# First batch of a fused attention and feed-forward kernel: four neighbouring tokens per partition, loads by pairs of heads, turned head by head with products

## Chip, cores, metric

One core of one Trainium2 chip. The metric is the time of the whole program on the device in microseconds (us), taken outside the profiler. A profile's span is about 1.8 us shorter than that time. The engines are called PE (matrix products; PEld is its weight load), ACT (scalar engine), DVE (vector engine) and POOL. Every comparison below is between runs of the fast state, with one exception that is named (a single run, e6).

## The reference, cut to what matters

```python
# x: (8, 8, 512, 64) batch, head, token, depth;  state: (8, 8, 32, 64);  all float32
scores  = x @ state.T / 8        ; a  = softmax(scores)  ; xread = a  @ state
scores2 = state @ x.T / 8        ; a2 = softmax(scores2) ; sread = a2 @ x
attn = concatenate([xread, sread], axis=tokens)          # 512 + 32 rows per batch
h = attn.reshape(4352, 512) @ w_in                       # w_in 512 x 2048, given as float64
out = (h * erf(softplus(h))) @ w_out                     # w_out 2048 x 512, float64
```

The weights come as float64 and are turned into float32 on the chip by ACT and DVE, step by step, while batch 0 is already in work. The order of tokens within a batch is free as long as the stores put the rows back.

## The kernel before, the parts that matter

Names: `st` is the state, `xT` is x turned so that a pair of heads (2 x 64) lies on the 128 partitions, `warm(n)` issues n products of the identity with itself, which keep PE busy. A plain product is two passes in the trace, a transpose one.

```python
x_t[0] = xin.tile([P, NC, H, D], F32, name="x")            # token 128*c + p on partition p
for c in range(NC):                                        # four quarters of the tokens
    (nc.scalar, nc.sync)[c % 2].dma_start(
        out=x_t[0][:, c], in_=x[0, :, P * c:P * c + P].rearrange("h p d -> p h d"))
for e in range(2):
    nc.sync.dma_start(out=st[:, 0, D * e:D * e + D], in_=...)
# ... then three weight loads of 1 MB on the sync queue, then warm(8)

def scored(b, xT):                                         # 8 products of 64*32 tiles, 512 columns
    s2 = [ps_at.tile([P, S], F32, name="at") for _ in range(2)]
    for i in reversed(range(NI)):
        for e in range(2):
            r, q = slice(D * e, D * e + D), slice(Ns * i, Ns * i + Ns)
            nc.tensor.matmul(out=s2[e][q, :], lhsT=st[r, b, q], rhs=xT[r, i, :], ...)
    return s2

def attention0(between):
    ...
    for c in 1, 0, 2, 3:
        if c == 2:
            warm(3)
        for i in range(NI):
            nc.tensor.transpose(out=xp[i][:, P * c:P * c + P],
                                in_=xt[:, c, 2 * i:2 * i + 2, :], identity=ident)
    for i in range(NI):
        (nc.scalar.copy, nc.vector.tensor_copy)[i % 2](xT[:, i, :], xp[i])
    states(range(1), ps_h, "h")                            # turn the state, copy by ACT
    s2 = scored(0, xT)
    between[0]()                                           # warm(32), first weight steps on ACT
    ...
    a = states_weights(0, s2, both)                        # DVE: transposes, maxima, ...
```

## Time and profile before

| | before |
|---|---|
| time, 4 runs | 732.15 us median (732.14 to 732.36) |
| span of the profiled run | 730.7 us |
| PE busy | 721.6 us (99%) |
| DVE busy from 11.5 to 31 us | 19.07 of 19.5 us |
| DVE's first transpose of scores starts | 11.57 us |
| first long group of PE products starts | 31.01 us |

### The profile page before, as it was taken

What the parts mean: (1) busy time and instruction counts of PE and PEld (TensorE: products, weight loads), DVE (VectorE), ACT (ScalarE), POOL (GpSimd) and SP (SyncE); (2) the same over time, 40 slices, a digit from 0 to 9 for tenths busy, and PEclk for the clock granted to TensorE, in tenths of its full rate; (3) what the DMA queues carried; (4) which work ended last, traced back from release to release, by engine and by line L of the source; (5) the groups of instructions that cost most, each with busy time, mean ns of one, the idle gap of its engine ahead of it and who ended that gap; (6) DMA issues with size and microseconds to landing.
All of it is one profiled execution on the core that took longest, in us unless ns stands there. A gap on an engine that the chain in (4) does not pass through costs nothing.

```text
span 730.7 us, 12128 instructions
## 1 busy us (share of the span) xinstructions
PE 721.6 (99%) x5016; PEld 588.0 (80%) x5016; DVE 524.0 (72%) x766; ACT 395.6 (54%) x498; POOL 0.7 (0%) x6
## 2 busy tenths in 40 slices
PE   8899999999999999999999999999999999999998
PEld 7434435889889888988989888988898899999996
DVE  4988887997798677867587669866686756674423
ACT  4898894665556444754455445544575434443340
POOL 0000000000000000000000000000000000000000
PEclk9999999999999999999999999999999999999999
DMA  7577842330153203310061104220111000000001
GB/s 234 174 216 241 224 94 58 87 59 30 19 99 67 50 1 66 80 30 30 1 144 27 33 1 94 60 44 9 38 50 30 30 1 30 1 30 1 30 1 29
DMA packets 139166, 46.40 MB, mean 64 GB/s; under 512 B 126696, under 2 KB 130536, under 8 KB 139112
## 3 DMA queue, kind: packets, MB, share of 16 engines
q1 hardware_dynamic: 136840, 44.92, 24.6%
q10 hardware_dynamic: 2272, 0.72, 0.5%
q8 instruction: 39, 0.64, 0.4%
q14 instruction: 15, 0.12, 0.1%
HBM read 33.03 MB, written 8.91 MB: 57 GB/s over the span
## 4 chain that ended last, share of the span: by engine, by line
PE 92%; DVE 2%; ACT 1%; issue 0%; ACTq 0%
PE o L600 50%; PE h L493 27%; PE o L550 7%; PE at L407 2%; PE h L407 1%; PE h L714 1%; PE at L197 1%; PE at L421 1%; PE h L277 1%; DVE s L727 0%; PE at L277 0%; DVE hs L721 0%; ACT L724 0%; DVE w_out L148 0%; ACT s L724 0%
## 5 line engine op out<-in xcount | busy, mean ns | idle before, releaser
L600 PE MATMUL o<-w_out,s 128*128 128x256 f32 x480 | 118.0, 380 | 0.0
L600 PE MATMUL o<-raw,hs 128*128 128x256 f32 x480 | 117.3, 382 | 0.0
L500 ACT ACTIVATE s<-hs 128x512 f32<-128x512 f32 x120 | 75.4, 630 | 74.3 <-DVE hs L501 74.0
L600 PE MATMUL o<-w_out,hs 128*128 128x256 f32 x480 | 114.1, 380 | 0.0
L600 PEld LDWEIGHTS o<-raw,hs 128*128 128x128 f32 x480 | 89.9, 190 | 22.6 <-issue 10.9
L501 DVE TENSOR_TENSOR hs<-hs,h 128x512 f32<-128x512 f32 x90 | 61.8, 687 | 62.6 <-PE h L493 62.4
L600 PEld LDWEIGHTS o<-w_out,hs 128*128 128x128 f32 x480 | 90.8, 190 | 16.3 <-issue 4.2
L600 PEld LDWEIGHTS o<-w_out,s 128*128 128x128 f32 x480 | 84.6, 191 | 7.9
L501 DVE TENSOR_TENSOR hs<-s,h 128x512 f32<-128x512 f32 x60 | 41.1, 685 | 67.6 <-PE h L493 67.1
L493 PEld LDWEIGHTS h<-aT,m 128*128 128x128 f32 x672 | 83.8, 192 | 4.3 <-issue 1.4
L493 PE MATMUL h<-aT,m 128*128 128x128 f32 x672 | 84.4, 275 | 0.0
L545 DVE TENSOR_TENSOR s<-s,hs 128x2048 f32<-128x2048 f32 (+1 forms) x31 | 68.8, 2218 | 20.4 <-ACT s L543 20.4
L504 ACT COPY s<-h 128x512 f32<-128x512 f32 x29 | 17.0, 585 | 107.7 <-PE h L493 107.7
L550 PE MATMUL o<-w_out,s 128*128 128x512 f32 x128 | 59.1, 600 | 0.6 <-DVE s L727 0.5
L493 PE MATMUL h<-sy,sx 128*128 128x128 f32 x448 | 59.4, 275 | 0.0
L493 PEld LDWEIGHTS h<-sy,sx 128*128 128x128 f32 x448 | 56.7, 192 | 2.1 <-issue 0.5
L543 ACT ACTIVATE s<-s 128x2048 f32<-128x2048 f32 x30 | 57.4, 1912 | 0.3
L509 ACT COPY hs<-h 128x512 f32<-128x512 f32 x29 | 17.0, 585 | 74.8 <-PE h L493 74.8
L600 PE MATMUL o<-raw,s 128*128 128x256 f32 x240 | 56.8, 379 | 0.0
L550 PEld LDWEIGHTS o<-w_out,s 128*128 128x128 f32 x128 | 23.1, 190 | 31.1 <-issue 25.8
L600 PEld LDWEIGHTS o<-raw,s 128*128 128x128 f32 x240 | 43.5, 190 | 4.7
L500 ACT ACT_TABLE_LOAD x31 | 39.8, 1283 | 0.5
(133 smaller groups left out, 915.4 us busy)
## 6 DMA issues: line engine op xcount, KB each, us to landing
raw<-in_moe_w_in_dram SPq DMA_DIRECT2D x8, 1024.0 KB, 5.7
raw<-in_moe_w_out_dram SPq DMA_DIRECT2D x8, 1024.0 KB, 4.8
xq<-in_x_dram SPq DMA_DIRECT2D x112, 64.0 KB, 2.2
x<-in_x_dram SPq DMA_DIRECT2D x56, 128.0 KB, 2.8
out_dram<-ot SPq DMA_DIRECT2D x18, 256.0 KB, 2.2
sc<-xT SPq DMA_DIRECT2D x112, 32.0 KB, 1.9
out_dram<-ot SPq DMA_DIRECT2D x28, 128.0 KB, 1.9
x<-in_x_dram ACTq DMA_DIRECT2D x2, 256.0 KB, 5.7
```

The lines of the kernel that those rows point to most:

```text
L197: on_pe = nc.tensor.matmul(out=s2[e][q, :], lhsT=st[r, b, q], rhs=xT[r, i, :], start=True, stop=True)
L277: nc.tensor.matmul(out=sr[q, e, :], lhsT=a2T[:, e, c, q], rhs=xt[:, c, 2 * i + e, :], start=(c == 0), stop=(c == NC - 1))
L407: nc.tensor.matmul(out=ps[k][e][q, :], lhsT=st[r, b, q], rhs=w_in[r, 2 * g:2 * g + 2, i, :], start=True, stop=True)
L493: last = nc.tensor.matmul(out=bank[:, q], lhsT=lhsT, rhs=rhs, start=(first and i == 0 and k == 0), stop=(i == GF - 1 and k == len(ops) - 1 ...
L500: nc.scalar.activation(out=s[:, k], in_=hs[:, k], func=ACTF.Softplus)
L501: add = lambda o, x, y: nc.vector.tensor_tensor(o, x, y, op=ALU.add)
L504: copy(m1, p)
L509: copy(c11, p)
L543: nc.scalar.activation(out=s, in_=s, func=ACTF.Erf)
L545: nc.vector.tensor_tensor(s[:, k], s[:, k], hs[:, k], op=ALU.mult)
L550: nc.tensor.matmul(out=acc[r], lhsT=gT[:, i, P * r:P * r + P], rhs=w_out[:, GF * g + i, :], start=(g == 0 and i == 0), stop=(g == NG - 1 a ...
L600: nc.tensor.matmul(out=acc[bank][:, E2 * c:E2 * c + E2], lhsT=lhs[:, i, :], rhs=rhs[:, g, i, :], start=(first and i == 0 and c == 0), stop ...
```

## The change

Its intent: each token's 64 numbers are 256 B, so the old load moved x in 4096 pieces of 256 B. With tokens 4p to 4p+3 on partition p, a head gives 1 KB per partition in one piece. Loading by pairs of heads also lets the first pair be turned, copied and scored while later pairs arrive. In the new layout the two heads of a token no longer lie side by side, so a transpose of 128 columns can't take them together, and each head is turned by a product with the identity.

```diff
-    x_t[0] = xin.tile([P, NC, H, D], F32, name="x")
-    for c in range(NC):
-        (nc.scalar, nc.sync)[c % 2].dma_start(
-            out=x_t[0][:, c], in_=x[0, :, P * c:P * c + P].rearrange("h p d -> p h d"))
-    for e in range(2):
-        nc.sync.dma_start(out=st[:, 0, D * e:D * e + D], in_=...)
+    x_t[0] = xin.tile([P, H, NC, D], F32, name="x").rearrange("p h c d -> p c h d")
+    def load_x0(queue, h, n):
+        queue.dma_start(out=x_t[0][:, :, h:h + n, :].rearrange("p c h d -> p h c d"),
+                        in_=x[0, h:h + n].rearrange("h (p c) d -> p h c d", c=NC))
+    for k in range(2):
+        for j, queue in enumerate((nc.scalar, nc.sync)):
+            load_x0(queue, 4 * k + 2 * j, 2)
+            if k == 0:
+                load_st0(queue, j)
 ...
-    def scored(b, xT):
+    def scored(b, xT, s2=None, pairs=tuple(reversed(range(NI)))):
 ...
-        (the loop over c with its 16 transposes, the four copies, states, scored(0, xT))
+        def turn(i):
+            for c in range(NC):
+                for e in range(2):
+                    nc.tensor.matmul(out=xp[i][D * e:D * e + D, P * c:P * c + P],
+                                     lhsT=xt[:, c, 2 * i + e, :], rhs=ident, start=True,
+                                     stop=True)
+            (nc.scalar.copy, nc.vector.tensor_copy)[i % 2](xT[:, i, :], xp[i])
+        turn(0)
+        turn(1)
+        states(range(1), ps_h, "h")
+        warm(2)
+        turn(2)
+        scored(0, xT, s2, (0, 1))
+        turn(3)
+        warm(2)
+        scored(0, xT, s2, (2, 3))
 ...
-        rows = out[TB * b:TB * b + S].rearrange("(c p) e -> c p e", p=P)
+        rows = out[TB * b:TB * b + S].rearrange("(p c) e -> c p e" if b == 0 else
+                                                "(c p) e -> c p e", p=P)
```

More of the change, by code (lines that the diff above doesn't have):

```diff
@@ L106, with load_st0 @@
     st = const.tile([P, B, P], F32, name="st")
-    x_t[0] = xin.tile([P, NC, H, D], F32, name="x")
-    for c in range(NC):
-        (nc.scalar, nc.sync)[c % 2].dma_start(
-            out=x_t[0][:, c], in_=x[0, :, P * c:P * c + P].rearrange("h p d -> p h d"))
-    for e in range(2):
-        nc.sync.dma_start(out=st[:, 0, D * e:D * e + D],
-                          in_=state[0].rearrange("(i e) n d -> e i n d", e=2)[e])
+    x_t[0] = xin.tile([P, H, NC, D], F32, name="x").rearrange("p h c d -> p c h d")
+    def load_x0(queue, h, n):
+        queue.dma_start(out=x_t[0][:, :, h:h + n, :].rearrange("p c h d -> p h c d"),
+                        in_=x[0, h:h + n].rearrange("h (p c) d -> p h c d", c=NC))
+    def load_st0(queue, e):
+        queue.dma_start(out=st[:, 0, D * e:D * e + D],
+                        in_=state[0].rearrange("(i e) n d -> e i n d", e=2)[e])
+    for k in range(2):
[3 more added lines that the diff above has]
+                load_st0(queue, j)
     def load_st():
@@ L188 @@
     marks = []
-    def scored(b, xT):
-        s2 = [ps_at.tile([P, S], F32, name="at") for _ in range(2)]
-        for i in reversed(range(NI)):
+    def scored(b, xT, s2=None, pairs=tuple(reversed(range(NI)))):
+        s2 = s2 or [ps_at.tile([P, S], F32, name="at") for _ in range(2)]
+        for i in pairs:
             for e in range(2):
@@ L299, in attention0 @@
         xp.append(ps_h.tile([P, S], F32, name="h"))
-        for c in 1, 0, 2, 3:
-            if c == 2:
-                warm(3)
-            for i in range(NI):
-                nc.tensor.transpose(out=xp[i][:, P * c:P * c + P],
-                                    in_=xt[:, c, 2 * i:2 * i + 2, :], identity=ident)
-        for i in range(NI):
+        s2 = [ps_at.tile([P, S], F32, name="at") for _ in range(2)]
+        def turn(i):
[4 more added lines that the diff above has]
+                                     stop=True)
             (nc.scalar.copy, nc.vector.tensor_copy)[i % 2](xT[:, i, :], xp[i])
+        turn(0)
+        turn(1)
         states(range(1), ps_h, "h")
-        s2 = scored(0, xT)
+        warm(2)
[4 more added lines that the diff above has]
+        scored(0, xT, s2, (2, 3))
         between[0]()
```

## The prediction

> **What bounds the kernel now.** I read the page first, then the stretches by engine, then the order of time of the first 32 us, then the waits, because the change touches only the load, the turn and the scores of batch 0, and the stores' row order. The page's head says what those can be worth at all:
>
> ```profile
> span 730.7 us, 12128 instructions
> PE 721.6 (99%) x5016; PEld 588.0 (80%) x5016; DVE 524.0 (72%) x766; ACT 395.6 (54%) x498; POOL 0.7 (0%) x6
> ```
>
> PE is busy for all but 9 us. A change before the first full stretch of PE work can only move that stretch earlier or later as a whole. The stretches (start and end; length; busy us of PE, PE weight load, DVE, ACT, POOL; clock; DMA share; GB/s) show where slack is:
>
> ```profile
> 11.50:31.00 19.50, 17.34 (x122) 11.61 (x122) 19.07 (x27) 15.97 (x21) 0.00 (x0) 1.00 0.52 184
> 31.00:52.00 21.00, 20.80 (x76) 8.57 (x77) 18.25 (x20) 19.17 (x23) 0.00 (x0) 1.00 0.73 220
> 52.00:130.00 78.00, 77.52 (x423) 35.71 (x422) 63.96 (x91) 60.33 (x87) 0.00 (x0) 1.00 0.57 149
> ```
>
> From 11.5 to 31 us DVE is the bound: 19.07 of 19.5 us, and the waits of DVE in that window hold nothing but the wait that starts it. PE is not the bound there: 64 of its 122 passes are fillers on the identity that keep its clock up. From 31 us PE is the bound. So the end is set by when DVE begins its first transpose of scores, at 11.57 us. What leads there, in order of time (start, length, engine, line, operation, count, idle before):
>
> ```profile
> 1.35 3.78 PE L169 MATMUL o<-ident 128*128 128x128 f32 x16 [1.35 <-POOL ident masks.py:199]
> 4.92 0.86 PE L304 MATMUL o<-ident,x 128*128 128x128 f32 x3
> 6.64 0.98 PE L169 MATMUL o<-ident 128*128 128x128 f32 x6
> 7.95 0.33 PE L304 MATMUL o<-ident,x 128*128 128x128 f32 x1 [0.32 <-DMA x<-in_x_dram]
> 9.47 0.68 DVE L307 COPY xT<-h 128x512 f32<-128x512 f32 x1
> 10.30 1.09 PE L197 MATMUL at<-xT,st 64*32 64x512 f32 x16 [0.78 <-DVE xT L307]
> 11.57 1.31 DVE L217 STREAM_TRANSPOSE xT<-at 128x512 f32<-128x512 f32 x2 [1.42 <-PE at L197]
> ```
>
> The reader should see three things. The last token quarter of x lands at 7.94 us and PE has waited for it (0.32 us, after a filler of 1 us): the start is DMA-bound at that point. From there to 11.57 it is a serial chain: 8 transposes, copies, scores. And a plain product counts two passes in the trace (warm(8) is x16), a transpose only one.
>
> **What the Trainium skill says.** (1) "TensorE: Matmul & The Clock Gate", section "Part 1: The HAM clock gate", gives half clock until about 3.4 us of sustained work. The trace agrees in kind: the fillers and the first transposes run at about 0.21 us per 128-column pass, later ones at 0.107 to 0.12, and the filler count per 0.2 us goes from 2 to 4 at about 7.0 us, although the granted clock reads 1.00 throughout. (2) "TensorEngine Tiling (Array Packing)", section "Feature Incompatibilities": column tiling excludes transpose mode for fp32, which is why turning heads one at a time must be done with products; its "Key Properties" say that changing the tiling mode drains the array. The trace shows such a cost: the weight combination between two 128*128 groups has 2 x 0.213 = 0.43 us of streaming per tile but takes 0.59, so about 0.08 us a switch. (3) "DMA: Bandwidth & Descriptors", section "Why small descriptors are slow (HBM only)": a 256 B descriptor pays 27% overhead. In the trace, x in 256 B pieces moves at 217 to 290 GB/s between 3 and 7 us, and the weights in 2 KB pieces at 400 to 430 between 9 and 14 us.
>
> **The change part by part.**
>
> Load. Four tokens per partition make each head's piece 1 KB instead of 256 B: 1024 pieces instead of 4096, for the same 1 MB and four transfers. Before, the transfers land at 4.83 us (issue 0.73 plus the shortest 4.1 to landing) to 7.94 us. Interpolating the time of a packet between 256 B and 2 KB at the two rates above, 1 KB pieces give some 370 to 390 GB/s (estimate). With first bytes at about 2.2 us as before, the first two pairs land about 4.4 to 4.8 us and the last two about 5.7 to 6.2. The data come about 2 us earlier, the first weight transfer too, since less is ahead of it. That takes the 7.94 wait away.
>
> Turn. 16 transposes (16 passes of 128 columns, over all 128 array columns) become 32 products (64 passes of 128 columns, each on half the columns). Two halves run side by side if the array treats them as it does the narrower products: in the read of tokens, 64 passes of 64 columns on 128*32 tiles take
>
> ```profile
> 87.48 1.03 PE at L277 x64
> ```
>
> where 64 x 0.053 = 3.4 us would be serial and a quarter is 0.85; so tiles do run together, plus some 0.18. For one turn of a pair: 16 passes / 2 x 0.107 = 0.86 us warm, 1.7 us cold. Four turns are 3.4 us warm against 16 x 0.122 = 1.95 us for the transposes: **PE's own work in the opening rises by 1.5 us**, more where it is cold. Copies are the same four, three of them now hidden.
>
> Scores. They split into two halves of 8 passes. Before, all eight tiles of 64*32 run together: 2 x 0.43 plus fill is 1.09. Each half still has two passes per tile of 0.43, so each half costs 0.86 plus fill: **one score time becomes two**, the first ahead of the last turn on PE.
>
> PE is in order, so I add its queue from the end of the unchanged fillers at 5.13 us:
> - turn 0, cold: 8 x 0.213 = 1.7, ends 6.85
> - turn 1, nearly all warm: 0.95, ends 7.8
> - switch, states' transpose and warm(2) (4 passes): 0.65, ends 8.45
> - turn 2 with a switch: 1.0, ends 9.45 (its data landed at about 6, no wait)
> - scores of pairs 0 and 1 with a switch: 0.95, ends 10.4
> - turn 3 with a switch: 1.0, ends 11.4
> - copy of the last pair on DVE: 0.1 to start plus 0.69, ends 12.2 (warm(2) lies beside it)
> - scores of pairs 2 and 3: 0.1 plus 1.05, ends 13.3; DVE begins at about 13.4
>
> Against 11.57 that is **+1.8 us**. The path no longer runs over DMA but over PE.
>
> Does the shift reach the end? DVE has no idle from 11.57 to 31 us, so it moves as a block; its weight steps wait for ACT's conversions, which come earlier with the data and not later. After 31 us PE idles 0.2 us in 21 and 0.5 us in 78, too little to absorb 1.8. The 64 filler passes move along (13.3 to 20.7) and end before the product at 19.64 + 1.8 that follows them. The stores of batch 0 go to rows four apart, but each row is still a 2 KB piece. The later read of x in its new layout still takes 64 contiguous numbers. So the sum: 732.15 + 1.8 = **733.95**, which I call 733.9.
>
> **The rivals.**
>
> (A) The gain is kept: the author's idea is that turns, copies and scores of early pairs hide under the loads, and that only one turn, one copy and half the scores follow the last landing. That tail is 1.0 + 0.8 + 1.15 + 0.15 = 3.1 us against 11.57 - 7.94 = 3.6 now. If PE were free at the last landing (6 us) DVE would begin about 9.1 and the time be 729.7; if PE is partly in the way, 731. Against it: PE's queue above contains nothing that waits for data after 5.1, and its tile-bound minimum without switches, 1.7 + 3 x 0.86 + 0.86 + 0.5 + 0.8 + 1.05, already puts DVE past 12.6.
>
> (B) The two halves of the array don't overlap in these products, for instance because the two passes of one product have to go in order: turns then cost 3.4 cold and 1.86 warm. The queue becomes 5.1, 8.3, 10.2, 10.8, 12.8, 13.7, 15.6, and DVE begins at about 17.5 (part of turn 0 warm saves 0.5): +5.5, 737.6. Against it stands the read of tokens, whose passes come in the same order and do overlap. For it: I have no row of a 128*64 tile.
>
> (C) The clock comes up one window later or earlier than 7.0 us. Before, PE waited for data at that time and was insensitive. Now turn 1 (and 2) would run cold: +0.9 to +1.7, so about 735.2; if earlier, -0.8, so 733.1.
>
> (D) The first pair lands later than 5.1 us, say 5.8, because the state pieces and two queues mix: all of PE's queue moves by 0.7, 734.6.
>
> **Range and chances.** I give the main sum, with (C) and (D) as its spread, some 75%, A 15%, B 10%. The 8-in-10 range is 732.0 to 735.8: below it lies most of A, above it B and the worst of C. A 2% verdict needs 14.6 us, the whole of the opening up to the scores and more; so within 2% is all but sure: faster 0.005, same 0.985, slower 0.01.
>
> **What would show each step.** In the profile after: x landing by about 6.2 us, with 350 GB/s or more in 3 to 5 us (load); no PE wait for x after the first turn; the turn's 16 passes taking 0.9 to 1.0 us warm and about 1.8 cold (overlap; 1.9 and 3.4 would be B); the last score half beginning near 12.3 with the last copy as its releaser; DVE's first transpose near 13.4, and the first long PE group of 24 passes, now at 31.01, near 32.8. The prediction is wrong in its sum if DVE's first transpose comes before 11.6, in its mechanism if PE waits there for x, and in its passing-on if DVE's start and that PE group move by different amounts or if the span moves by less than they do.

## The result and the profile after

| | before | after |
|---|---|---|
| time, 4 runs | 732.15 us (732.14 to 732.36) | 734.86 us (733.97 to 735.66) |
| span of the profiled run | 730.7 | 733.0 |
| DVE's first transpose of scores starts | 11.57 | 13.96 |
| first long group of PE products starts | 31.01 | 33.37 |

Ratio 1.0036, 95% interval 1.0019 to 1.0053. (A ratio is the mean time of one kernel's fast runs over the mean of the other's of the same rounds, so not quite the ratio of the medians.) The changed kernel is slower by 2.7 us, and its runs spread over 1.7 us, where those of the kernel before spread over 0.2.

The changed kernel in order of time (start, length, engine, line, operation, count, idle before). These lines answer to those of before in the prediction:

```profile
5.07 3.16 PE L314 MATMUL o<-ident,x 128*64 128x128 f32 x32
8.16 0.33 PE L191 MATMUL h<-ident,st 128*128 128x128 f32 x1
8.86 1.09 PE L314 MATMUL o<-ident,x 128*64 128x128 f32 x16
9.89 1.06 PE L206 MATMUL at<-xT,st 64*32 64x512 f32 x8
10.88 1.09 PE L314 MATMUL h<-ident,x 128*64 128x128 f32 x16
12.02 0.69 DVE L317 COPY xT<-h 128x512 f32<-128x512 f32 x1 [3.05 <-PE h L314]
12.54 0.36 PEld L206 LDWEIGHTS at<-xT,st 64*32 64x32 f32 x8
12.55 1.27 PE L206 MATMUL at<-xT,st 64*32 64x512 f32 x8
13.96 1.31 DVE L226 STREAM_TRANSPOSE xT<-at 128x512 f32<-128x512 f32 x2 [1.24 <-PE at L206]
...
33.37 1.12 PE L568 MATMUL o<-w_out,s 128*128 128x512 f32 x2 [0.24 <-DVE s L746]
```

Before, PE waited for the last quarter of x until 7.94 us. In this trace no PE line carries a wait for x: PE goes from turn to scores to turn without a gap. The one late wait of the opening is DVE's 3.05 us for the last turn. The copy of that turn ends at 12.71, 2.56 us after the last copy of before (9.47 + 0.68 = 10.15).

The stretch that follows, from each kernel's start of the DVE block, is nearly a copy of that of before. DVE is busy 18.69 of 19.5 us (about 0.46 us of this stretch lies ahead of the block's start), and it waits for nothing between 13.96 and the first long PE group:

```profile
13.50:33.00 19.50, 17.63 (x126) 11.80 (x122) 18.69 (x26) 13.42 (x19) 0.00 (x0) 1.00 0.34 114
```

So in this trace the loss is made entirely in the first 14 us: 13.96 - 11.57 = 2.39 us there, 33.37 - 31.01 = 2.36 at the first long PE group, 733.0 - 730.7 = 2.3 at the end.

### The profile page after: what moved, and what is told of

It reads as the page before. It is cut to its first block, busy times and chain, and to the rows that moved or that the text cites. A ratio compares the mean times of both kernels' runs of the same rounds, so it can differ in the third digit from the quotient of the medians.

```text
span 733.0 us, 12227 instructions
## 1 busy us (share of the span) xinstructions
PE 725.1 (99%) x5066; PEld 590.2 (81%) x5066; DVE 524.1 (71%) x766; ACT 395.6 (54%) x498; POOL 0.7 (0%) x6
## 4 chain that ended last, share of the span: by engine, by line
PE 90%; DVE 3%; ACT 2%; issue 1%; DVEq 0%; ACTq 0%
PE o L618 49%; PE h L511 27%; PE o L568 7%; PE at L425 2%; PE h L425 1%; PE h L733 1%; PE at L206 1%; PE at L439 1%; PE h L286 1%; DVE s L746 0%; PE at L286 0%; DVE hs L740 0%; ACT L743 0%; DVE w_out L157 0%; DVE xT L357 0%
```

## The experiments

Twelve kernels ran on the chip, and all gave the reference's result. "DVE start" is the start of DVE's first transpose of scores in that run's trace. Times are medians with the lowest and highest in brackets; "before" is that of the same rounds. The rounds ran on four chips (e1 to e4; e5 to e8; e9 to e11; e12); their medians of before lie between 732.33 and 732.36, so runs of different rounds are compared directly. The diffs below are shortened.

| run | what | time | before | DVE start | first long PE group | span |
|---|---|---|---|---|---|---|
| e1 | the changed kernel again | 734.73 (734.07 to 735.03) | 732.36 | 14.06 | 33.47 | 733.1 |
| e2 | new tokens, pairs kept side by side, transposes | 732.65 (732.15 to 732.82) | 732.36 | 10.94 | 30.36 | 730.4 |
| e3 | changed loads, regrouping copies, transposes | 733.69 (731.73 to 735.30) | 732.36 | 14.46 | 33.93 | 733.5 |
| e4 | changed, scores undivided | 733.58 (732.81 to 733.80) | 732.36 | 12.81 | 32.22 | 731.9 |
| e5 | changed, x on one queue | 734.11 (733.85 to 734.73) | 732.35 | 13.18 | 32.63 | 732.3 |
| e6 | changed, state loads last (one run) | 735.41 | 732.35 | 14.55 | 33.97 | 733.6 |
| e7 | e3 with x on one queue | 731.33 (730.78 to 731.41) | 732.35 | 10.51 | 29.97 | 729.6 |
| e8 | e7 with 256 B pieces | 731.97 (731.83 to 732.07) | 732.35 | 10.99 | 30.43 | 730.1 |
| e9 | e5, scores undivided | 733.43 (732.49 to 733.55) | 732.33 | 12.59 | 32.04 | 731.7 |
| e10 | e5, turns ordered by head | 735.70 (735.22 to 736.22) | 732.33 | 14.52 | 33.95 | 733.6 |
| e11 | before, x on one queue | 732.13 (732.05 to 732.51) | 732.33 | 11.19 | 30.61 | 730.2 |
| e12 | e7, states behind x | 730.65 (730.61 to 731.31) | 732.34 | 9.64 | 29.13 | 728.9 |

Read the last three columns first. In these twelve traces and the two of before and after, the long PE group starts 19.41 to 19.49 us after DVE's start. The span ends 719.0 to 719.5 us after it. Whatever an experiment does to the opening, the end moves by the amount by which DVE's start moves, within 0.13 us of before's 719.13. The exception is e2, 0.33 longer: its shift is still whole at DVE's last instruction (726.44 us against 727.09), and 0.3 us is lost after it, in the last stores. From here on, only the way to DVE's start is asked about.

The two theories at the outset: the loss is **PE's own added work** (four times the passes for the turns, each on half the array, and the scores twice), partly run at half clock; or it is **something else the change brought** (the token order, the loads, the stores).

### e1: the changed kernel again

No edit.

> The changed kernel itself, to learn its spread and where its tensor clock comes up. My theory: the first turns of the changed kernel run partly at half clock, and the moment at which the clock comes up (about 7.0 us in the profile before, about 7.5 in the profile after) differs from run to run; each us that it comes later costs half a us. So the runs spread between about 733.9 and 735.7, while the kernel before, which waits for data until 7.94 us, stays within 0.3 of 732.15. In this run's trace the start of DVE's first transpose of scores minus 11.57 equals the span minus 730.7 within 0.1 us. Rival (the spread is chance of the chip and hits both kernels, or comes after the opening): the kernel before spreads as much, or the span and DVE's start do not move together.

The spread came back (1.0 us here, against 0.4 for 11 runs of before on the same chip), and the span followed DVE's start: +2.49 and +2.4. The first two turns, the same 32 passes from the same start, took different times in different traces of this code. After, e1, e5 (which differs only in its queues):

```profile
5.07 3.16 PE L314 MATMUL o<-ident,x 128*64 128x128 f32 x32
```
```profile
5.06 2.60 PE L314 MATMUL o<-ident,x 128*64 128x128 f32 x32
```
```profile
5.06 2.23 PE L313 MATMUL o<-ident,x 128*64 128x128 f32 x32
```

The stretches of PE alone (start and end, length, busy and passes touched, clock, DMA share, GB/s) show why. In the profile after, two equal stretches of 0.4 us at 5.6 and 6.6 us hold the same few passes, and only the one at 7.6 holds more:

```profile
5.60:6.00 0.40, 0.40 (x8) 1.00 1.06 371
6.60:7.00 0.40, 0.40 (x8) 1.00 1.05 407
7.60:8.00 0.40, 0.40 (x12) 1.00 1.05 410
```

while in e5 a faster rate is there already at 6.4:

```profile
5.20:5.60 0.40, 0.40 (x6) 1.00 1.03 318
6.40:6.80 0.40, 0.40 (x14) 1.00 1.05 404
```

The rate doubled at about 7.5 us after, 6.5 in e1 and 5.8 in e5, read from where the pass count rises in stretches of 0.2 us; this document calls it the clock coming up, though the "1.00" in the clock column shows none of it. It can come earlier still: in e11 and e12 the first fillers, the same 16 passes that take 3.78 us elsewhere, were shorter, and the rate doubled at about 4.2 and 4.6 us:

```profile
1.35 3.40 PE L169 MATMUL o<-ident 128*128 128x128 f32 x16 [1.35 <-POOL ident masks.py:199]
1.35 3.58 PE L177 MATMUL o<-ident 128*128 128x128 f32 x16 [1.35 <-POOL ident masks.py:199]
```

What was not expected is a second source of spread: e1 had its first turns done 0.56 us earlier than the profile after, yet its DVE started 0.1 us later. PE waited for the third pair of x, which had not landed before 8.97 us:

```profile
8.97 1.09 PE L314 MATMUL o<-ident,x 128*64 128x128 f32 x16 [0.59 <-DMA x<-in_x_dram]
```

That load was issued on the scalar queue at 2.43 us, so it took 6.5 us. Between 7 and 8 us the sync queue (q1) moves weights with nearly all engine time, and the scalar queue (q10) still has 23 packets under way (packets, MB, share of the engines):

```profile
q1 hardware_dynamic: 167, 0.33, 93.2%
q10 hardware_dynamic: 23, 0.02, 5.2%
```

### e2: the new tokens without the products

```diff
-    x_t[0] = xin.tile([P, H, NC, D], F32, name="x").rearrange("p h c d -> p c h d")
+    x_t[0] = xin.tile([P, NC, H, D], F32, name="x")      # loads head by head
-  32 products                                            # in turn(i)
+  nc.tensor.transpose(out=xp[i][:, P*c:P*c+P], in_=xt[:, c, 2*i:2*i+2, :], identity=ident)
-  warm(2), scored (0, 1), warm(2), scored (2, 3)
+  warm(2), scored (0, 1, 2, 3) once, at the end
```

> Four tokens per partition kept, but the tile keeps the heads of a token side by side, so that pairs of heads are turned by 16 transposes as before (one pass each), scores undivided, no fillers after the first eight; loads head by head, with 256 B pieces on the chip's side. My theory (PE's own added work is what costs): the last head lands at about 7 to 8 us, DVE's first transpose of scores starts at 10.5 to 11.5, time 731.1 to 732.1, and the spread is small again. Rival (the new token order or the order of loads costs by itself, for instance through the stores to every fourth row): 734 or more although the products are gone.

DVE started at 10.94, inside the expected window, and the profiled run took 732.16. The median of 732.65 missed the expected 731.1 to 732.1: it is level with before, ratio 1.0003 (0.9991 to 1.0016). The small spread did not come either (0.67 us). The rival is out: with the new token order, the new stores and the order by pairs all kept, the 2.4 us are gone. (The expectation said no fillers after the first eight; in fact one warm(2) stayed.) The simplest version, transposes on the changed layout, does not build (it never ran): the build refuses a stationary operand with more than one free dimension, and two heads 1 KB apart have two. That, and not only the column tiling that the prediction named, is why the change needs products.

### e3: the changed loads, two heads laid side by side by copies

```diff
+  xg = act.tile([P, 4, S], F32, name="hs")
+  for i in range(NI):
+      (nc.vector.tensor_copy, nc.scalar.copy)[i % 2](
+          xg[:, i].rearrange("p (c e d) -> p c e d", c=NC, e=2), xt[:, :, 2*i:2*i+2, :])
-  32 products
+  nc.tensor.transpose(out=xp[i][:, P*c:P*c+P], in_=xg[:, i, P*c:P*c+P], identity=ident)
-  the fillers and the divided scores
+  scored(0, xT, s2, (0, 1, 2, 3)) once, at the end
```

> The changed loads exactly (1 KB pieces by pairs of heads), then DVE and ACT, idle at that time, copy each pair so that its two heads lie side by side, and 16 transposes and undivided scores follow. My theory: pairs land at 4.3 to 6 us, copies of 0.4 to 0.7 us end by about 6.7, transposes end at about 7.5, DVE's first transpose of scores starts at 9.5 to 10.3: time 730.1 to 730.9, faster than both. Rival (DMA still bounds, or what DVE starts earlier is lost again because the first weights are not converted): DVE's start may be earlier but the time is 732 or more, with a new wait on ACT or the weight transfer in the DVE block.

A miss, and the most useful one. The runs lie between 731.73 and 735.30. The trace is of the slowest, and DVE's copy of the third pair shows what it stood on:

```profile
9.69 0.43 DVE L319 COPY hs<-x 128x512 f32<-128x512 f32 x1 [4.67 <-DMA x<-in_x_dram]
```

The third pair, issued on the scalar queue at 2.72, landed at 9.69, while the fourth, on the sync queue, was there by 7.05. PE then stood idle for 2.92 us. Of the eight transposes left, four still ran at the high rate (0.66 us) and four at the low one (0.99), and the scores took 2.73 us. So the sentence in the prediction that the last two pairs land at 5.7 to 6.2 us is wrong. The profile after shows it too, in its times from issue to landing: the third pair was issued at 2.44 us and took 5.1, so it landed at about 7.5. Only, PE was not ready for that pair before 8.86 there, so that nothing waited.

### e4: the scores undivided

```diff
-        scored(0, xT, s2, (0, 1))
         turn(3)
         warm(2)
-        scored(0, xT, s2, (2, 3))
+        scored(0, xT, s2, (0, 1, 2, 3))
```

> The changed kernel with the scores in one piece after the last turn. My theory: a half of the scores costs PE as much as the whole (two passes of 0.43 us per tile), so the first half's 1.0 us leaves the queue and nothing comes in its place but the switch of mode: DVE starts 0.8 to 1.1 us earlier than in the changed kernel, time 733.8 to 734.1 at the same clock. Rival (the halves run half as long, and the first half is hidden as was meant): the time rises by 0.3 to 0.5.

1.15 us faster than e1 in the median (733.58 against 734.73), with DVE's start 1.25 us earlier. The rival is out: dividing the scores costs and hides nothing. The undivided scores take as long in the trace as one half does in the profile after:

```profile
11.40 1.27 PE L206 MATMUL at<-xT,st 64*32 64x512 f32 x16
```

### e5 and e6: which queue, and what stands last in it

e5: the four loads of x on the sync queue, in order, both state loads on the scalar queue. e6: on each queue both loads of x, then one state load.

```diff
-    for k in range(2):
-        for j, queue in enumerate((nc.scalar, nc.sync)):
-            load_x0(queue, 4 * k + 2 * j, 2)
-            if k == 0:
-                load_st0(queue, j)
+    for j in range(4):                      # e5
+        load_x0(nc.sync, 2 * j, 2)
+    for j in range(2):
+        load_st0(nc.scalar, j)
```

> The changed kernel with all four loads of x on the sync queue, in order and ahead of the first weights, and both state loads on the scalar queue. Theory W: in the changed kernel the third pair lands late (8.97 us in e1, 8.86 in e4, 9.69 in e3) because on the scalar queue it shares the engines with the first weights of the sync queue. Then here all pairs land by 5.8 us, PE never waits for x after the first turn, and DVE's start is set by PE alone: 13.4 to 14.0 depending on when the clock comes up, time 733.9 to 734.8, with a smaller spread; so it stays slower than before by 1.6 to 2.4 us, because PE's queue is the bound. Rival: the transfers are slow by themselves with this layout; the last pair then lands at 8 us or later here too.

> The changed kernel with both x loads of each queue ahead of the state load, so that the third pair is issued on the scalar queue at about 1.3 us instead of 2.4 us. Theory W (shared with the weights): its bytes are asked for before the weights, so it lands by about 6, one look 733.9 to 734.9. Rival L (a load on the scalar queue is late whatever is issued when): it lands at 7.5 us or later, as before.

e5: no wait for x any more; the longest of the four loads took 4.8 us to land instead of 6.5. The expected landing of all pairs by 5.8 us did not come: the last load, issued at about 2.3, landed at about 7.1, before PE needed it. The median fell by 0.62 us against e1 and stayed 1.76 above before. So the late third pair is worth up to 0.6 us (the runs of e1 and e5 overlap; PE's wait for it was 0.59 us in e1's trace, 0.26 in e4's and nothing in the profile after), and the rest is PE. The expected smaller spread did not come: 0.9 us against 1.0, which leaves the clock as the likely main source of the spread (argued from the turns' lengths above, not forced by an experiment).

e6: the third pair, now issued at about 1.3 us, made PE wait no more; no load of x took more than 5.0 us. The late one was now the state, last on the scalar queue:

```profile
8.76 0.33 PE L191 MATMUL h<-ident,st 128*128 128x128 f32 x1 [1.12 <-DMA st<-in_state_dram]
```

So it is not x or its layout that is slow. What stood last on the scalar queue while the sync queue had a megabyte of weights in flight landed late, and the time with it (735.41, a single run, above the expected 733.9 to 734.9). That the weights are what delays it is argued: no run takes them away.

### e7 and e8: the regrouping copies with the loads put right, and the size of the pieces

e7 is e3 with e5's queues and all four copies on DVE. e8 is e7 with "(c p)" in place of "(p c)" in the load and in the stores, so the pieces are 256 B again.

> e3 (1 KB pieces, copies that lay pairs of heads side by side, 16 transposes) with x on the sync queue ahead of the weights, and all four copies on DVE. Theory: pairs land at 3.6 to 5.7 us, copies of 0.43 us end by 6.2, PE turns from 5.1 to 7.8 or 8.7 (depending on the clock) without a gap, DVE's first transpose starts at 9.8 to 10.7: 0.9 to 1.8 us less than before of the same chip, so 730.5 to 731.4, and a spread well under that of e3 (3.6 us). Rival: DVE's start comes that early but the span follows by less, because the first weights (landing near 10 us or later) then hold up the DVE block.

> e7 with the old assignment of tokens to partitions, so that x moves in 256 B pieces again; nothing else differs. Theory (the piece size is what the four tokens per partition buy): 1 MB at 220 to 290 GB/s, so the last pair lands at 6.6 to 7.4 instead of 5.7, DVE's start is 0.7 to 1.5 us later than in e7. Rival (the load is latency and issue, not pieces): within 0.3 us of e7.

e7 beats before: 731.33 against 732.35, ratio 0.9983 (0.9970 to 0.9996), DVE's start at 10.51. The time fell by 1.02 us, as DVE's start did (1.06 against the 11.57 of before), so the rival (first weights in the way) is out. ACT did wait 0.91 us for the first weights, but DVE needs them only at 14.10.

e8 is 0.64 us slower than e7, and no run of one reaches into those of the other. DVE's start is 0.48 later: less than the expected 0.7 to 1.5, more than the rival's 0.3. So the piece size counts, for less than was thought. Between 3 and 6 us all transfers together moved 308, 264 and 360 GB/s in e7, and 267, 223 and 218 in e8. The last row of e7 holds the first weights, in 2 KB pieces; of x alone, the sync queue moved 0.54 MB in e7 and 0.44 in e8 between 3 and 5 us:

```profile
3.00:4.00 1.00, 1.00 (x6) 1.00 (x6) 0.39 (x1) 0.82 (x1) 0.00 (x0) 1.00 1.07 308
4.00:5.00 1.00, 1.00 (x7) 1.00 (x6) 0.30 (x2) 0.00 (x0) 0.00 (x0) 1.00 0.85 264
5.00:6.00 1.00, 1.00 (x7) 1.00 (x6) 0.47 (x2) 0.00 (x0) 0.00 (x0) 1.00 1.07 360
```
```profile
3.00:4.00 1.00, 1.00 (x6) 1.00 (x6) 0.00 (x0) 0.79 (x1) 0.00 (x0) 1.00 1.21 267
4.00:5.00 1.00, 1.00 (x7) 1.00 (x6) 0.43 (x1) 0.00 (x0) 0.00 (x0) 1.00 1.26 223
5.00:6.00 1.00, 0.74 (x6) 0.51 (x4) 0.43 (x1) 0.26 (x1) 0.00 (x0) 1.00 1.27 218
```

### e9 and e10: the two terms of PE's queue, with the loads out of the way

e9 is e5 with e4's edit. e10 is e5 with the loops of a turn exchanged:

```diff
-            for c in range(NC):
-                for e in range(2):
+            for e in range(2):
+                for c in range(NC):
```

> e5 (changed kernel, x on one queue) with the scores undivided, as in e4. Theory: the first half of the scores (1.0 us plus switches) leaves PE's queue and, since no wait for x takes its place, the time falls by 1.0 to 1.3 us against e5: 732.8 to 733.2. Rival (part of e4's gain of 1.15 us was the clock or the late pair): it falls by less than 0.8.

> e5 with the products of a turn ordered by half of the array (all four of one head, then all four of the other), so that neighbours on PE's queue use the same half. Theory (overlap needs neighbours on different halves; e5's turns take 8 x 0.107 us because heads alternate): a warm turn costs about 1.7 instead of 0.95 us, the two cold ones together about 5 instead of 2.2 to 3.2, so DVE starts 2.5 to 4 us later: 736.6 to 738.1. Rival (PE pairs them in whatever order within a turn): no change against e5, 734.1 within 0.5.

Against e5, e9 fell by 0.68 us only, by the medians: below the expected 1.0 to 1.3, and by that measure the rival's case. Its trace, however, had a late clock: the first two turns took 2.95 us, against 2.23 in e5's. Read from PE's queue, where the clock is up in both, the term is there in full. From the start of turn 2 to the start of turn 3 it is 2.01 us in e5 (8.09 to 10.10) and 0.93 in e9 (8.64 to 9.57), so the half scores cost 1.08 us. What is left, 1.1 us above before with neither divided scores nor a wait for x, is put down to the products.

e10 slowed by 1.59 us against e5, less than the expected 2.5 to 4 and far from the rival's nothing. A turn at the high clock, from its start to that of the scores behind it, takes 1.51 us in e10 and 1.02 in e5. The first group is of e10, the second of e5:

```profile
8.47 1.58 PE L313 MATMUL o<-ident,x 128*64 128x128 f32 x16
9.98 0.63 PE L205 MATMUL at<-xT,st 64*32 64x512 f32 x4
```
```profile
8.09 1.09 PE L313 MATMUL o<-ident,x 128*64 128x128 f32 x16
9.11 0.63 PE L205 MATMUL at<-xT,st 64*32 64x512 f32 x4
```

Sixteen passes one after the other would be 16 x 0.107 = 1.71 us and a full overlap 0.86, each plus a switch. So alternating halves overlap nearly fully, and with four neighbours on the same half some overlap remains. How PE arranges that stays open. Part of the miss is the clock, too: it came up early in that trace, at about 5.5 us, so the first two turns together took 2.77 us and not about 5.

### e11: the kernel before with only its queues changed

```diff
-        (nc.scalar, nc.sync)[c % 2].dma_start(out=x_t[0][:, c], ...)
+        nc.sync.dma_start(out=x_t[0][:, c], ...)
-        nc.sync.dma_start(out=st[:, 0, D * e:D * e + D], ...)
+        nc.scalar.dma_start(out=st[:, 0, D * e:D * e + D], ...)
```

> The kernel before with only its queues changed: all four loads of x on the sync queue, the states on the scalar queue. Theory (e7's gain comes from the earlier landing that 1 KB pieces and the queue give, at equal work of PE): the last 256 B quarter lands at about 7.2 to 7.9 us as in e8, where the last copy waited until 7.88, so the time is within 0.4 of before. Rival (the queue alone is worth e7's 1.0 us): 731.4 or less.

732.13 against 732.33, ratio 0.9999 (0.9985 to 1.0012): the queue alone is worth little, and the rival is out. The last quarter landed at 8.0 us, just outside the expected window. Of e7's 1.0 us, the queue alone gives 0.2 (e11) and the queue with the copies but 256 B pieces 0.4 (e8); the larger pieces without the queue made it slower in the median (e3, whose copies were also shared with ACT).

### e12: nothing on the second queue

```diff
-        load_st0(nc.scalar, j)
+        load_st0(nc.sync, j)                # behind the four loads of x
         turn(1)
-        states(range(1), ps_h, "h")
         turn(2)
         turn(3)
+        states(range(1), ps_h, "h")
```

> e7 with the state loads behind x on the sync queue (nothing on the scalar queue at all) and the states' transpose behind the four turns. In e7 the fourth pair landed at 7.00 us and the states at 7.37, PE waiting 0.55 us for them. Theory (two queues in flight at once delay whichever is last in its own): the fourth pair lands by 6 us, PE has no gap, and DVE starts at 9.8 to 10.3 instead of 10.51: time 730.5 to 731.1. Rival (the states' smaller pieces then land after 8 us, just before the scores): DVE's start as in e7 or later, 731.3 or more.

730.65, ratio to before 0.9979 (0.9966 to 0.9993): the fastest of all. DVE's start came at 9.64, a little before the expected window. The fourth pair was copied from 6.53 us on instead of 7.00, later than the expected 6, and PE still has gaps: 0.53 us for the third pair at 6.33 and 0.35 for the state's copy. The scores run undivided. Two queues in flight were the theory; this trace also has the earlier clock shown under e1, so how much of the 0.68 us between e7 and e12 is the queue is not shown. Its lines:

```profile
6.53 0.43 DVE L318 COPY hs<-x 128x512 f32<-128x512 f32 x1 [0.26 <-DMA x<-in_x_dram]
8.24 1.26 PE L205 MATMUL at<-xT,st 64*32 64x512 f32 x16 [0.35 <-ACT st L191]
9.64 1.31 DVE L225 STREAM_TRANSPOSE xT<-at 128x512 f32<-128x512 f32 x2 [1.24 <-PE at L205]
```

## Why the prediction held, and where it was off

The main sum was slower by 1.8 us. Measured were 2.7 us (first rounds) and 2.4 us (e1), inside the range but 0.6 to 0.9 us above the sum. By the prediction's own steps, with the profile after:

| step | predicted | measured |
|---|---|---|
| turns 0 and 1 end | 7.8 | 8.16 |
| states and warm(2) | 0.65 | 0.70 |
| turn 2 | 1.0 | 1.03 |
| scores of pairs 0 and 1 | 0.95 | 0.99 |
| turn 3 | 1.0 | 1.02 |
| copy of the last pair | 0.8 | 0.81 |
| end of that copy to DVE's start | 1.2 | 1.25 |
| DVE's start | 13.4 | 13.96 |

- **The mechanism was right in the main**: PE's queue took the place of the wait for x. Its two added costs were the products (e9, without divided scores, stays 1.1 us above before; e2 and e7, without both, lose no time) and the divided scores (1.15 us in e4, 1.08 us of PE's queue in e9). By the prediction's own sign ("in its mechanism if PE waits there for x") it held whole in the first profile and only in part in e1, where PE waited 0.59 us.
- **The passing-on was right** to a tenth of a microsecond in nearly all fourteen traces.
- **The mis-sized term is the clock.** "Turn 1, nearly all warm" took the clock to come up at 7.0 us, as in the profile before. In the profile after it came up at about 7.5, which is 0.36 of the 0.56 us that were missing; the other 0.2 are tenths spread over the later steps. The prediction had this as its rival (C), but as the outcome of a rare window. It is a part of every run: the moment lay between 5.8 and 7.5 us in the traces of the same instructions. Before, PE waited for data at that time, which would explain why that kernel's runs hardly spread; it is argued, not shown (e2 waits for x until 7.88 us and spreads over 0.67).
- **The load step failed.** "The last two about 5.7 to 6.2" did not hold: the third pair landed at about 7.5 us in the profile after, 8.97 in e1, 8.86 in e4, 9.69 in e3. The sign "350 GB/s or more in 3 to 5 us" failed in the profile after as well (362 and 179, mean 270):

```profile
3.00:4.00 1.00, 1.00 (x7) 1.00 (x6) 0.00 (x0) 1.00 (x1) 0.00 (x0) 1.00 1.03 362
4.00:5.00 1.00, 1.00 (x6) 0.84 (x4) 0.00 (x0) 0.14 (x1) 0.00 (x0) 1.00 0.82 179
```

  The rate of 370 to 390 GB/s for 1 KB pieces was interpolated towards the weights' 2 KB pieces. Of the 371 packets between 4 and 5 us, 258 were under 512 B: nearly all are the states' pieces, which stood between the loads of x. And nothing was allowed for weights in flight on the other queue. (The landing times don't follow from the figures named beside them: 2.2 us plus 1.05 MB at 380 GB/s gives 5.0; some 0.7 to 1.2 us were added unsaid.) The failed step cost up to 0.6 us (e5). That "no PE wait for x after the first turn" came out right in the first profile is luck of that run: it was wrong in e1 (0.59 us) and e4 (0.26).
- **Rival (B)**, no overlap of the two halves, was wrong for the order that the change uses (1.02 us a turn), and half true for the other order (1.51, e10). **Rival (A)**, the gain kept, is what e7 and e12 reach by other means: leave PE its transposes and put the loads right.

## What to carry to other kernels

When an early stage waits for data, don't pay for earlier data with work on the engine that does the stage next: ask where that engine's queue ends without any wait, at the clock that it will have then. In this kernel a product that fills half of the array was not half a product (a pair turned by products took 1.02 us, by four transposes 0.49 in e2), and splitting a group of products that run side by side doubled their time (1.27 us for 8 passes as for 16). Loads that are needed first did best at the head of one queue, with nothing large in flight on another.

## What the Trainium skill lacked or had wrong

- "TensorE: Matmul & The Clock Gate", Part 1, says full clock comes around 4 us into sustained activity, ±500 ns run to run. The runs show a wider range: PE was busy from 1.35 us without a gap, and the rate doubled at about 4.2 (e11), 5.8 (e5), 6.5 (e1) and 7.5 us (after), that is 2.9 to 6.2 us after its first pass. The profile's clock column read 1.00 all along.
- "DMA: Bandwidth & Descriptors", "Issuing engines are not separate DMA queues", says that loads from several engines interleave and that issuing from several saves only issue time. That section lacks the cost: a 256 KB load that was last on the scalar queue, with weights in flight on the sync queue, took 6.5 us to land (e1), and with all of x on the sync queue the slowest took 4.8 (e5) and 5.6 (e9).
- The same page, "Why small descriptors are slow (HBM only)", gives 27% overhead for 256 B. The runs agree roughly: 0.54 MB of x in two us with 1 KB pieces against 0.44 with 256 B (23% more), worth 0.64 us of 732 here. That section lacks the rate of 1 KB pieces, which the prediction put at 370 to 390 GB/s: x came at 270, with the states' loads beside it (e7, 3 to 5 us).
- "TensorEngine Tiling (Array Packing)" doesn't say that the order of instructions decides how far column tiles overlap: a turn of sixteen 128*64 passes took 1.02 us with halves alternating and 1.51 with four of one half in a row (e5, e10).
